# A fused attention and geglu kernel: three regroupings of maxima, copies and loads

## Chip, core and metric

The kernel runs on one core of a Trainium2 chip. The metric is the device time of one execution in microseconds, taken as the median of several runs; beside it stands one execution recorded by the hardware profiler, from which all rows come. In the rows PE is TensorE's matmuls and PEld its weight loads, DVE is VectorE, ACT ScalarE, POOL GpSimd and SP SyncE, which issues the DMAs.

## The reference

Sequence of 2048 tokens, width 576, 32 heads of 18, feed-forward width 4608, all in fp32.

```python
def _A_ref(x, wqkv, wo):                       # attention, H = 32, Dh = 18
    qkv = (x @ wqkv).reshape(B, S, 3, H, Dh).transpose(2, 0, 3, 1, 4)
    q, k, v = qkv[0], qkv[1], qkv[2]
    scores = jnp.einsum("bhqd,bhkd->bhqk", q, k) * (Dh ** -0.5)
    p = softmax(scores)
    o = jnp.einsum("bhqk,bhkd->bhqd", p, v)
    return o.transpose(0, 2, 1, 3).reshape(B, S, D) @ wo

def _B_ref(x, w_gate, w_up, w_down):           # geglu
    return (gelu(x @ w_gate) * (x @ w_up)) @ w_down

xn = layernorm(x)
out = x + _A_ref(xn, ...) * silu(_B_ref(xn, ...))
```

## The kernel before

**Values in two parts.** Each fp32 operand of the feed-forward and of the output projection is split into a high part that the matmul takes at full rate and a low part, the rest; a product is three matmuls (high by high, high by low, low by high). `split` and `cut` make these parts on the vector engines.

**Stages.** A prologue does the layer norm, q, k and v (to about 199 us). Then the feed-forward runs as 144 sections: four blocks of 512 tokens, in each 18 row groups r, in each two halves g. A section is 27 pairs of matmuls (`gate_up`, L423) into two PSUM banks, pg and pu, each pair with a gate row and an up row. Most sections share one pair of banks (tag "f"), so the next section's first matmul waits until `activate` has read them (L432, L433, L436, L437). After every second section, an even one, the products with w_down (`downs`, L534, in the first block also L521) are added into M on VectorE (L538, L523).

**Attention between the pairs.** Sections 0 to 10 are the lead: they carry the row maxima of the first unit of heads and queries and some of the second (`max_pair`: matmuls L767 into one of three ring buffers in PSUM, a reduce L768 on VectorE), four or five to a section from n=2 on. Sections 11 to 138 carry attention: eight score and eight maximum steps placed between the pairs by `spread`, then 32 value matmuls (L821), then the products of w_down where due. `spread` takes a number `tail`: so many of the specials are put behind the last pair instead of between pairs.

**Block changes.** Behind sections 35, 71 and 107 the next block's x is needed. It comes in three tiles `xd[k]`, each of a high and a low part, by DMA into partitions 0 to 63; `copy_xd` doubles them into partitions 64 to 127 (ScalarE the high part, GpSimd the low part). A slice (64x512) is a third of a tile. Pair 9k is the first that needs tile k, and hooks put work ahead of a pair by its number. `finish` ends a section: sums and cuts of the activations (L461, L451, L452) on GpSimd in the middle stretch. `sums_b` (L486 to L488) forms the sums of two row groups of w_down, and the pieces of these sums are stored; later blocks load them again (`t_piece`, L479).

**Epilogue.** Sections 139 to 143 carry no attention. The output projection runs between and behind them in 16 steps, one for each 128 tokens: `ready` splits the attention output (`split_o`) and computes the gate of the step after (`gate`: Tanh L944 on ScalarE, L945 on VectorE), `project_o` does the matmuls (L954), multiplies by the gate (L960) and adds x (L967); `load_xy` loads x and the feed-forward result yy of a later step. `load_wo` loads the output weights in five DMAs. `rec` is the reciprocal of the last unit's sums; its store (L848) is a task behind section 139.

**Order.** TensorE runs in program order, and so does SyncE from the attention on. The other engines are ordered by the planner of the framework, except that instructions marked `keep_in_program_order` keep theirs among themselves.

Of the kernel before, what the change touches and what calls it, by code (L numbers as in the profile page):

```python
# [10 lines left out]
AF = mybir.ActivationFunctionType  # L11
ALU = mybir.AluOpType
# [5 lines left out]
P = 128  # L18
# [5 lines left out]
HR = 64  # L24
NC = D // HR
XG = 3
NG = NC // XG
# [10 lines left out]
G = 2  # L38
# [24 lines left out]
def f(ap):  # L63
    return ap.bitcast(F32)
# [15 lines left out]
def kernel(ctx: ExitStack, tc: tile.TileContext, x, wqkv, wo, w_gate, w_up, w_down, out):  # L80
    nc = tc.nc
    x = x.rearrange("b s d -> (b s) d")
# [60 lines left out]
            out.append(t)  # L143
        return out

    def copy_xd(x, keep=lambda i: i, i=slice(None)):

        keep(nc.scalar.activation(x[0][HR:P, i], f(x[0])[0:HR, i], AF.Copy))
        keep(nc.gpsimd.tensor_copy(x[1][HR:P, i], x[1][0:HR, i]))  # L149


    def after(what, before, reason):
# [9 lines left out]
    with tc.tile_pool(name="pro", bufs=1) as pro, tc.tile_pool(name="pps", bufs=1, space=PSUM) as pps:  # L162
# [160 lines left out]
        t = ORDER[0]  # L323
# [29 lines left out]
        for b in range(NB):  # L353
# [43 lines left out]
    FF = {"w": ahead, "xd": XD, "down": [], "gates": [], "n": 0, "hooks": {}, "next": {}, "raw": {},  # L397
          "M": ffn.tile([P, 7, 2, DC], F32, name="M"),
          "A": [ffn.tile([P, 7, TH], F32R, name=m) for m in ("ah", "al")],
          "T": ffn.tile([P, 2, 7, DC], F32R, name="T")}  # L400
# [80 lines left out]
    def sums_b(raw):  # L481

        keep = tc.keep_in_program_order
        q = raw.rearrange("p g (c d) -> p (g c) d", c=2)
        t = ffn.tile([P, 5, DC], F32, name="tsum")
        keep(nc.gpsimd.tensor_tensor(t[:, 1:3], q[:, 0:4:2], q[:, 1:4:2], op=ALU.add))  # L486
        keep(nc.gpsimd.tensor_tensor(t[:, 3:5], q[:, 0:2], q[:, 2:4], op=ALU.subtract))
        keep(nc.gpsimd.tensor_tensor(t[:, 0], q[:, 0], q[:, 3], op=ALU.add))  # L488
        FF["b"] = q, t
# [79 lines left out]
    def section(specials=(), tag="f", slots=False, tail=0):  # L569

        n = FF["n"]
        FF["n"] += 1
        b, r = divmod(n // G, NR)
        g = n % G
        keep = tc.keep_in_program_order
        pairs, pg, pu = gate_up(tag)
        hooks, FF["hooks"], FF["next"] = FF["hooks"], FF["next"], {}

        def hook(i, what):
            hooks.setdefault(i, []).append(what)  # L580

        for i in range(n + 1, min(n + 3, NF)):
            if i not in FF["raw"]:
                FF["raw"][i] = load_gu(i % (NR * G))
        nxt = FF["raw"].pop(n + 1, None)
        one = split_ap if n + 1 < ATT.start else split
        if nxt:
            for k in range(NG - 1):
                split_gu(nxt, k, one)
        if n == 0:  # L590
            load_rawd(0)
        if g == 0 and (b, r) in FORMED:
            raw = FF["rawd"]
            hook(12, lambda: sums_b(raw))
        new = n + 1 < NF and (n + 1) % (NR * G) == 0
        xd = []
        if new:
            for k in range(NG - 1):
                hook(9 * k + 9, lambda k=k: xd.append(load_xd(b + 1, k)))
        for p in spread(pairs, specials, 1 if slots else None, hooks, tail):  # L600
            p()
        if nxt:
            split_gu(nxt, NG - 1, one)
        FF["w"] = nxt
        FF["act"] = activate(pg, pu, g, n < ATT.stop)
        if g > 0 or n not in ATT:
            FF.pop("last", lambda: None)()
        if new:
            xd.append(load_xd(b + 1, NG - 1))
            copy_xd(xd[0], keep)  # L610
            for k in range(1, NG):
                for i in range(XG):
                    FF["hooks"].setdefault(8 * k - 7 + 3 * i, []).append(lambda k=k, i=i: copy_xd(xd[k], keep, i))
            FF["xd"] = xd

    def downs(then={}):
# [93 lines left out]
    with tc.tile_pool(name="att", bufs=1, reuse_waits="tile") as att:  # L710
# [145 lines left out]
        for n, m in enumerate(FIRST):  # L856
            none = [lambda: None]
            lead = [lambda s=s: max_pair(*divmod(s, NS)) for s in range(slot, slot + m)]
            section((n == 2) * 5 * none + lead + (m > 0 and n != 2) * none, "ring" if n == 1 else "f",
                    tail=3 * (m > 0 and n % G == 0))  # L860
            if slot + m >= NS > slot:
                max_neg(0, tc.keep_in_program_order)
                max_store(0)
                FF["hooks"].setdefault(10, []).append(lambda: max_end(0))
            slot += m
            while n > 0 and chunk < KB and chunk * SLOTS <= slot + SLOTS:
                load_k(chunk)
                chunk += 1
            if n == 0:
                load_k(0)  # L870
                load_q(0)
            if n == 3:
                load_q(1)
            if n >= len(FIRST) - 2:
                load_v(n - len(FIRST) + 2)
            downs()
            finish()
        scaled = 0
        for n in range(NU * NA):
            u, i = divmod(n, NA)  # L880
# [31 lines left out]
    with tc.tile_pool(name="epi", bufs=1, reuse_waits="tile") as epi:  # L912
# [3 lines left out]
        def load_wo():  # L916
            keep = tc.keep_in_program_order
            nc.gpsimd.memset(f(OW[1])[HR:P, KT, :], 0.0)
            for i, w in enumerate(OW):
                keep(nc.sync.dma_start(f(w)[:, 0:KT, :], wos[i, 0:R0, :].rearrange("(k p) n -> p k n", p=P)))  # L920
                for a in range(2 - i):
                    keep(nc.sync.dma_start(f(w)[HR * a:HR * a + HR, KT, :], wos[i, R0:D, :]))
# [9 lines left out]
        def load_xy(b, j):  # L932

            rows = slice(b * TB + j * P, b * TB + (j + 1) * P)
            XY[b, j] = [epi.tile([P, D], F32, name=m, bufs=n) for m, n in (("xx", 4), ("yy", 3))[0:2 - (b == NB - 1)]]
            for t, a in zip(XY[b, j], (x, ys)):
                nc.sync.dma_start(t, a[rows, :])

        def gate(b, j):

            if b < NB - 1:
                yy = XY[b, j][1]
                th = epi.tile([P, D], F32, name="th")
                nc.scalar.activation(th, yy, AF.Tanh, scale=0.25)  # L944
                nc.vector.scalar_tensor_tensor(yy, th, 1.0, yy, op0=ALU.add, op1=ALU.mult)  # L945

        def project_o(b, j):

            po = ring("po")
            oh, ol = o = OP.pop((b, j))  # L950
            terms = [(k, x, w) for k in range(KT) for x, w in ((0, 0), (0, 1), (1, 0))] + [(KT, 0, 0), (KT, 0, 1)]
            for c in range(2):
                for m, (k, x, w) in enumerate(terms):
                    nc.tensor.matmul(po[:, c, 0:DC], o[x][:, k, :], OW[w][:, k, DC * c:DC * c + DC], start=(m == 0),  # L954
                                     stop=(m == len(terms) - 1))
            xx = XY[b, j][0]
            if b < NB - 1:
                t = XY[b, j][1]
                t2 = t.rearrange("p (c d) -> p c d", c=2)
                nc.vector.scalar_tensor_tensor(t2, t2, 0.25, po[:, :, 0:DC], op0=ALU.mult, op1=ALU.mult)  # L960
            else:
                t = epi.tile([P, D], F32, name="last", tag="yy", bufs=3)
                for c in range(2):
                    m = QUARTERS[2 * (j // 2) + c][2]
                    nc.vector.scalar_tensor_tensor(t[:, DC * c:DC * c + DC], FF["M"][:, m, j % 2], 0.25, po[:, c, 0:DC],
                                                   op0=ALU.mult, op1=ALU.mult)
            (nc.vector if (b, j) == groups[-1] else nc.gpsimd).tensor_tensor(xx, xx, t, op=ALU.add)  # L967
            outs.append((b * TB + j * P, xx))

        groups = [(b, j) for b in range(NB) for j in range(TB // P)]  # L970
        load_xy(*groups[0])
        load_wo()
        load_xy(*groups[1])
        n, outs = 0, []

        def ready():
            if n == len(groups):
                return
            b, j = groups[n]
            split_o(b, j)  # L980
            gate(b, j)
            if b < 2 and j == TB // P - 1:
                load_o(b + 2)

# [14 lines left out]
        for i in range(ENDS):  # L999
            section([], "ring" if i % 2 else "f")  # L1000
            if i == 1:
                ready()
            downs()
            finish()
            if i == 0:
                todo.pop("rec")[0]()
            if 0 < i <= NU - scaled:
                scale(scaled + i - 1)
                store_scale(scaled + i - 1)
            if i < NU - scaled:  # L1010
                load_scale(scaled + i)
            for k in range(GROUPS[i]):
                step()
# [4 lines left out]
        for i, c, m in QUARTERS:  # L1018
            t = ffn.tile([P, 2, DC], F32, name="tg", tag=("h0", "h1")[c], bufs=2 - c)
# [33 lines left out]
```

## Time and profile before

| | us |
|---|---|
| median of 3 runs | 2641.1 |
| lowest and highest | 2637.55 and 2644.84 |
| the profiled execution's own time | 2643.16 |
| its span | 2641.4 |
| its mean granted TensorE clock | 0.991 of full speed |

Busy shares of the span count time in which an instruction runs; matmuls are pipelined, and their ends are modelled. A row of a timeline gives start, duration, engine, line, operation, the tile written and the tiles read, a count where like instructions were joined, and in brackets the idle time of the engine before it and who ended that. The granted clock is the share of full speed that TensorE was allowed in a stretch of time.

### The profile page before, as it was taken

To read this page: it belongs to the slowest core of one execution; us is meant where nothing else is said; L and a number is where in the kernel's file an instruction comes from. 1 tells how busy PE (TensorE), PEld (TensorE's weight loads), DVE (VectorE), ACT (ScalarE), POOL (GpSimd) and SP (SyncE) were. 2 spreads that over 40 slices of the span, in tenths; PEclk is the share of its full clock that TensorE was granted. 3 is DMA by queue.
4 is the path that set the end of the run, shared out by engine and by line. 5 is a ranking of instruction groups with operands and counts; after the bars stand their busy time and mean duration, and the time that the engine had idled before them with its cause. 6 is when DMAs were issued, how large, how long until landed. Compare 5 with 4: busy or idle time off the path is not lost.

```text
span 2641.4 us, 52882 instructions
## 1 busy us (share of the span) xinstructions
PE 2572.5 (97%) x20548; PEld 1847.5 (70%) x20548; DVE 2164.7 (82%) x2459; ACT 1476.0 (56%) x1779; POOL 1580.3 (60%) x1603
## 2 busy tenths in 40 slices
PE   9999999999989999999999999999999999999988
PEld 8887766666656666666666666666666666667777
DVE  5325799999978988999988989888888988897467
ACT  3224366666667655555566655555566555555622
POOL 2115588888877855555566555555556555555642
PEclk9999999999999999999999999999999999999998
DMA  8875365555555566666675666555566655554683
GB/s 259 261 240 138 88 178 157 164 161 161 164 164 170 163 168 154 168 156 171 164 179 158 166 166 157 157 158 158 157 148 192 165 144 154 151 147 138 190 252 122
DMA packets 407881, 442.88 MB, mean 168 GB/s; under 512 B 106700, under 2 KB 286412, under 8 KB 407632
## 3 DMA queue, kind: packets, MB, share of 16 engines
q1 hardware_dynamic: 407632, 439.50, 60.3%
q8 instruction: 163, 2.67, 0.4%
q14 instruction: 86, 0.70, 0.1%
HBM read 344.12 MB, written 95.26 MB: 166 GB/s over the span
## 4 chain that ended last, share of the span: by engine, by line
PE 86%; DVE 7%; DMA 3%; ACT 1%; POOL 1%; issue 1%; SPq 1%; DVEq 0%; POOLq 0%; ACTq 0%
PE pg L423 20%; PE py L534 14%; PE acc L821 13%; PE pu L423 11%; PE pe L804 9%; PE pm L767 8%; PE po L183 7%; DVE mx L768 1%; DMA T<-ts 1%; PE po L954 1%; DVE m L777 1%; PE py L521 1%; DVE h L440 1%; DVE h L433 1%; DVE accs L827 1%
## 5 line engine op out<-in xcount | busy, mean ns | idle before, releaser
L805 ACT ACTIVATE pT<-pe 128x1024 f32<-128x1024 f32 x1024 | 1047.8, 1026 | 617.7 <-PE pe L804 583.6
L768 DVE TENSOR_REDUCE mx<-pm 128x2 f32<-128x1024 f32 x1024 | 1221.8, 1224 | 188.8 <-PE pm L767 170.3
L423 PE MATMUL pu<-xd,wh 64*128 64x512 f32 x2538 | 929.0, 397 | 6.8 <-POOL xd L149 5.2
L423 PE MATMUL pg<-xd,wh 64*128 64x512 f32 x2538 | 928.3, 397 | 4.7 <-ACT t L436 4.7
L423 PEld LDWEIGHTS pg<-xd,wh 64*128 64x128 f32 x2538 | 469.1, 185 | 120.5 <-issue 62.9
L423 PE MATMUL pg<-xd,wl 64*128 64x512 f32 x1269 | 497.3, 392 | 1.1 <-POOL wl L115 1.1
L423 PE MATMUL pu<-xd,wl 64*128 64x512 f32 x1269 | 497.0, 392 | 0.0
L423 PEld LDWEIGHTS pu<-xd,wh 64*128 64x128 f32 x2538 | 469.2, 185 | 35.1 <-POOL xd L149 6.8
L108 POOL TENSOR_SCALAR wh<-raw 128x384 fp32r<-128x384 f32 x402 | 214.5, 536 | 444.7 <-PE pu L423 313.4
L821 PE MATMUL acc<-pT,VS 128*32 128x512 f32 x4096 | 467.3, 597 | 0.0
L804 PE MATMUL pe<-QT,KA 64*128 64x512 f32 x2048 | 418.6, 398 | 21.1 <-DVE mx L768 8.6
L110 POOL TENSOR_TENSOR wl<-raw,wh 128x384 fp32r<-128x384 f32 x402 | 410.2, 1023 | 27.7
L767 PE MATMUL pm<-KA,QT 64*128 64x512 f32 x2048 | 416.1, 395 | 4.7 <-ACT pT L805 3.6
L534 PE MATMUL py<-T,ah 128*128 128x288 f32 x1876 | 385.5, 301 | 14.9 <-DMA T<-ts 9.3
L538 DVE TENSOR_TENSOR M<-py,M 128x576 f32<-128x576 f32 x448 | 339.0, 758 | 34.5 <-PE py L534 19.9
L534 PEld LDWEIGHTS py<-T,ah 128*128 128x128 f32 x1876 | 301.8, 190 | 70.1 <-issue 54.5
L452 POOL TENSOR_TENSOR al<-h,ah 128x512 fp32r<-128x512 f32 (+1 forms) x139 | 286.4, 2061 | 59.5 <-ACT ah L449 42.3
L821 PEld LDWEIGHTS acc<-pT,VS 128*32 128x32 f32 x4096 | 120.2, 110 | 277.9 <-issue 231.3
L804 PEld LDWEIGHTS pe<-QT,KA 64*128 64x128 f32 x2048 | 195.1, 184 | 144.8 <-DVE mx L768 32.9
L534 PE MATMUL py<-T,al 128*128 128x288 f32 x938 | 277.6, 296 | 0.0
L423 PEld LDWEIGHTS pg<-xd,wl 64*128 64x128 f32 x1269 | 235.2, 185 | 32.0 <-POOL wl L115 2.0
L423 PEld LDWEIGHTS pu<-xd,wl 64*128 64x128 f32 x1269 | 235.3, 185 | 14.4
(154 smaller groups left out, 2962.1 us busy)
## 6 DMA issues: line engine op xcount, KB each, us to landing
T<-ts SPq DMA_DIRECT2D x98, 576.0 KB
KA<-qk SPq DMA_DIRECT2D x768, 72.0 KB
T<-ts SPq DMA_DIRECT2D x98, 432.0 KB
raw<-in_B_w_gate_dram SPq DMA_DIRECT2D x144, 288.0 KB
raw<-in_B_w_up_dram SPq DMA_DIRECT2D x144, 288.0 KB
ts<-T SPq DMA_DIRECT2D x36, 576.0 KB
VS<-vs SPq DMA_DIRECT2D x128, 152.0 KB
qk<-t SPq DMA_DIRECT2D x72, 256.0 KB
```

The source lines that it names most:

```text
L108: first = nc.gpsimd.tensor_scalar(hi, raw, 1.0, 1.0, op0=ALU.mult, op1=ALU.mult)
L110: keep(nc.gpsimd.tensor_tensor(lo, raw, f(hi), op=ALU.subtract))
L183: nc.tensor.matmul(o, st, m, start=(i == 0), stop=(i == len(terms) - 1))
L423: nc.tensor.matmul(o, w[1 + wp][k][rr, c, :], xd[k][xp][rr, c, :], start=(i == 0), stop=(i == len(terms) - 1))
L452: keep(two.tensor_tensor(lo, raw, f(hi), op=ALU.subtract))
L534: nc.tensor.matmul(py[:, t, 0:DC], h[:, i, tt], T[:, w, k], start=n == 0, stop=n == 2)
L538: nc.vector.tensor_tensor(M[:, m], py[:, :, 0:DC], M[:, m], op=ALU.add)
L767: nc.tensor.matmul(pm[:, a], QS[u, r][rr, t * P:(t + 1) * P], KS[(u * NA + c) % KB][r][rr, :], start=True, stop=True)
L768: nc.vector.tensor_reduce(MX[u][:, 2 * r:2 * r + 2, t, c], pm, axis=AX.X, op=ALU.max)
L804: nc.tensor.matmul(pe[:, a], KS[(u * NA + c) % KB][r][rr, t * P:(t + 1) * P], QS[u, r][rr, :], start=True, stop=True)
L805: nc.scalar.activation(PT[u, kt][:, 2 * r:2 * r + 2, :], pe, AF.Exp, scale=SCALE)
L821: nc.tensor.matmul(ACC[u][32 * a:32 * a + 32, :], VS[(u * NA + c) % VB][:, v:v + 32], pt[:, a, :], start=first, stop=last, skip_group_chec ...
```

## The change

The diff regroups work in three stages.

In the lead, the last three specials of a section (two maxima and an empty one) are placed behind the pairs in sections with odd n instead of even n.

At a block change, `copy_xd` gets an argument for the part. Before, tile 0 was copied whole at the end of the old block's last section, tile 1 in slices ahead of pairs 1, 4 and 7, and tile 2 in slices ahead of pairs 9, 12 and 15, on both engines. After, ScalarE copies tiles 0 and 1 whole at the section's end, and tile 2 in slices ahead of pairs 4, 8 and 12; GpSimd copies all nine slices at the section's end, ahead of the sums of `finish`. The hook of `sums_b` goes from 12 to 22 in a block's first section that has one (r == 0).

In the epilogue, the loads of the output weights and of the first two steps' x and yy are given out behind section 139, after its `finish` and before the store of rec, instead of ahead of section 139. `gate` moves from `ready` into `project_o`, one step later. The adds of L967 run on VectorE in all steps; before, GpSimd did them in all but the last.

```diff
-    def copy_xd(x, keep=lambda i: i, i=slice(None)):
+    def copy_xd(x, part, keep=lambda i: i, i=slice(None)):
 
-        keep(nc.scalar.activation(x[0][HR:P, i], f(x[0])[0:HR, i], AF.Copy))
-        keep(nc.gpsimd.tensor_copy(x[1][HR:P, i], x[1][0:HR, i]))
+        if part == 0:
+            keep(nc.scalar.activation(x[0][HR:P, i], f(x[0])[0:HR, i], AF.Copy))
+        else:
+            keep(nc.gpsimd.tensor_copy(x[1][HR:P, i], x[1][0:HR, i]))
...
             raw = FF["rawd"]
-            hook(12, lambda: sums_b(raw))
+            hook(22 if r == 0 else 12, lambda: sums_b(raw))
...
         if new:
             xd.append(load_xd(b + 1, NG - 1))
-            copy_xd(xd[0], keep)
-            for k in range(1, NG):
+            for k in range(2):
+                copy_xd(xd[k], 0, keep)
+            for i in range(XG):
+                FF["hooks"].setdefault(4 + 4 * i, []).append(lambda i=i: copy_xd(xd[NG - 1], 0, keep, i))
+            for k in range(NG):
                 for i in range(XG):
-                    FF["hooks"].setdefault(8 * k - 7 + 3 * i, []).append(lambda k=k, i=i: copy_xd(xd[k], keep, i))
+                    copy_xd(xd[k], 1, keep, i)
             FF["xd"] = xd
...
             section((n == 2) * 5 * none + lead + (m > 0 and n != 2) * none, "ring" if n == 1 else "f",
-                    tail=3 * (m > 0 and n % G == 0))
+                    tail=3 * (m > 0 and n % G == 1))
...
             xx = XY[b, j][0]
+            gate(b, j)
             if b < NB - 1:
...
-            (nc.vector if (b, j) == groups[-1] else nc.gpsimd).tensor_tensor(xx, xx, t, op=ALU.add)
+            nc.vector.tensor_tensor(xx, xx, t, op=ALU.add)
             outs.append((b * TB + j * P, xx))
 
         groups = [(b, j) for b in range(NB) for j in range(TB // P)]
-        load_xy(*groups[0])
-        load_wo()
-        load_xy(*groups[1])
         n, outs = 0, []
...
             b, j = groups[n]
             split_o(b, j)
-            gate(b, j)
             if b < 2 and j == TB // P - 1:
...
             finish()
             if i == 0:
+                load_wo()
+                load_xy(*groups[0])
+                load_xy(*groups[1])
                 todo.pop("rec")[0]()
```

## The prediction

> **What bounds the kernel now.** I read the page first, then windows by stage, then what the matmuls waited for, then timelines around the places that the diff touches. The page's first row, and the chain that ended last by engine:
>
> ```profile
> PE 2572.5 (97%) x20548; PEld 1847.5 (70%) x20548; DVE 2164.7 (82%) x2459; ACT 1476.0 (56%) x1779; POOL 1580.3 (60%) x1603
> PE 86%; DVE 7%; DMA 3%; ACT 1%; POOL 1%; issue 1%; SPq 1%; DVEq 0%; POOLq 0%; ACTq 0%
> ```
>
> TensorE is busy for 97% of the span. The diff leaves its matmuls as they are, so it can move the 3% of idle time and the time lost to a lower granted clock, and nothing else. Where these lie shows in windows of the lead, of the sections of attention up to the first block change, of two block changes and of the epilogue (start:end, length, then busy time of PE, PEld, DVE, ACT and POOL with instructions, granted clock, DMA share, GB/s):
>
> ```profile
> 212.00:333.00 121.00, 109.21 (x854) 90.71 (x856) 92.81 (x109) 43.75 (x76) 64.61 (x56) 1.00 0.43 111
> 333.00:742.00 409.00, 408.24 (x3408) 279.84 (x3404) 372.09 (x403) 271.97 (x314) 336.77 (x323) 1.00 0.57 163
> 742.00:786.00 44.00, 34.96 (x244) 23.39 (x236) 31.48 (x31) 23.73 (x29) 36.09 (x34) 0.92 0.55 153
> 1361.00:1400.00 39.00, 33.86 (x242) 23.77 (x236) 30.01 (x30) 21.50 (x25) 26.50 (x27) 0.91 0.71 197
> 2501.00:2641.40 140.40, 116.88 (x848) 108.12 (x846) 102.19 (x132) 31.82 (x45) 46.48 (x38) 0.91 0.63 196
> ```
>
> In the sections between block changes nothing is left to win (0.8 us idle in 409). The lead idles 11.8 us, the two block changes 9.0 and 5.1 us, the epilogue 23.5 us, and in the last three the clock sags too. Those are the three places of the diff. The waits of TensorE (what waited, who released it: total us, times, the longest):
>
> ```profile
> PE py L534 <- DMA T<-ts: 9.3, 1, 9.3
> PE pu L423 <- POOL xd L149: 5.2, 3, 3.7
> PE py L534 <- DVE M L538: 4.7, 1, 4.7
> PE py L521 <- DVE mx L768: 3.1, 5, 0.6
> ```
>
> One wait for a piece of w_down's sums (T), three for GpSimd's copies of x, 3.7 the longest, one for a VectorE add in the epilogue, and five short ones in the lead.
>
> **Part 1, the lead: +8 us.** Four reduces follow in each section of four maxima; with the tail, three of them stand on VectorE in front of L433 and L437, which read the section's two PSUM banks. An even section (n=4) ends so, then the end of an odd one (n=5):
>
> ```profile
> 244.32 0.39 PE L423 MATMUL pu<-xd,wh 64*128 64x512 f32 x1
> 244.56 0.63 PE L767 MATMUL pm<-KA,QT 64*128 64x512 f32 x3
> 244.52 3.49 DVE L768 TENSOR_REDUCE mx<-pm 128x2 f32<-128x1024 f32 x3 [1.96 <-PE pm L767]
> 248.52 0.68 DVE L437 TENSOR_TENSOR t<-t,pg 128x512 f32<-128x512 f32 x1
> 245.80 0.53 PE L521 MATMUL py<-T,ah 128*128 128x288 f32 x2 [0.62 <-DVE mx L768]
> ...
> 259.44 0.39 PE L423 MATMUL pu<-xd,wh 64*128 64x512 f32 x1
> 261.90 0.49 PE L423 MATMUL pu<-xd,wh 64*128 64x512 f32 x1 [0.40 <-DVE t L437]
> ```
>
> In n=4 the pairs end at 244.71 (244.32 + 0.39), and L437 gives the banks back at 249.20 (248.52 + 0.68): 4.49 us later. It costs nothing, since w_down's matmuls (L521) run meanwhile; they wait only 0.62 for a ring buffer. In n=5, without a tail, the next section goes on at 261.90, 2.07 us behind the end of its pairs at 259.83. Nothing but the next section follows an odd one, and that needs the two banks. So with the tail there, TensorE resumes 4.49 instead of 2.07 behind the pairs, +2.4. Two maxima, four matmuls in some 0.5 us (by x3 in 0.63), leave the pairs and run inside the gap: +2.0 net. Odd sections with maxima are n=3, 5, 7, 9: **+8.0**. Gone are the five waits of L521, **-3.1**. What is late next is the odd section's Tanh and sums; their products are read only behind the following even section, some 10 us on, and cost nothing.
>
> The gap may also cost clock. Of its 4.0 us behind the tail's maxima one matmul fills 0.5. What such gaps did in two other places (windows of about one step of the clock, as above):
>
> ```profile
> 776.70:780.10 3.40, 1.26 (x12) 0.74 (x10) 3.40 (x3) 0.76 (x1) 3.40 (x3) 1.00 0.02 5
> 780.10:783.50 3.40, 3.40 (x20) 2.67 (x18) 1.86 (x3) 2.05 (x2) 3.40 (x4) 0.51 0.00 0
> ...
> 281.80:285.20 3.40, 2.32 (x22) 1.57 (x18) 2.66 (x3) 1.05 (x2) 1.83 (x2) 1.00 0.35 104
> ```
>
> After 1.26 busy of 3.40 the next 3.40 run at 0.51, which loses 3.40 x 0.49 = 1.7 us. At 2.32 busy of 3.40, in the lead, the windows beside it keep 1.00. A gap of 4.0 with 0.5 busy lies nearer the first, but part of it can fall into two such windows and part of a slow stretch may run beside another wait; between 0 and 1.7 I take half, 0.85 x 4 = **+3.4**. The lead: 8.0 - 3.1 + 3.4 = **+8** (bounds +5 and +12).
>
> The Trainium skill ("TensorE: Matmul & The Clock Gate", its part on the clock gate) lets the clock fall only after a whole idle window of about 3.4 us; by that the lead would come to +5, since the matmul in the gap breaks it. The rows above differ from it: 1.26 us of work stood in the window ahead of the slow one.
>
> **Part 2, block changes: -10 us.** At the first (n=36 begins near 742), GpSimd, ScalarE and TensorE, then TensorE at the second, and the window behind each of the two waits:
>
> ```profile
> 743.68 1.73 POOL L149 CAST xd<-xd 64x512 fp32r<-64x512 f32 x3 [0.47 <-DMA xd<-xhs]
> 749.59 2.94 POOL L452 TENSOR_TENSOR al<-h,ah 128x1280 fp32r<-128x1280 f32 x1
> 758.12 0.79 POOL L488 TENSOR_TENSOR tsum<-rawd 128x288 f32<-128x288 f32 x1
> 758.97 0.60 POOL L149 CAST xd<-xd 64x512 fp32r<-64x512 f32 x1
> 742.82 0.60 ACT L825 ACTIVATE accs<-acc 128x512 f32<-128x512 f32 x1
> 744.73 0.63 ACT L148 ACTIVATE xd<-xd 64x512 fp32r<-64x512 f32 x1
> 759.63 0.79 PE L423 MATMUL pu<-xd,wh 64*128 64x512 f32 x1 [3.73 <-POOL xd L149]
> ...
> 1370.33 0.55 PE L423 MATMUL pu<-xd,wh 64*128 64x512 f32 x1 [1.28 <-POOL xd L149]
> ```
> ```profile
> 759.65:763.10 3.45, 3.45 (x17) 1.05 (x21) 1.91 (x2) 1.11 (x2) 2.98 (x4) 0.51 0.55 174
> 1370.70:1374.10 3.40, 3.40 (x20) 2.65 (x18) 1.42 (x2) 2.47 (x3) 3.23 (x6) 0.51 1.05 320
> ```
>
> The last slice copy (758.97) stands on GpSimd behind the unit's sums (L452 ends at 752.5) and the sums of the next rows of w_down (L488 ends at 758.9). The last pair waits 3.73 for it, and the stretch after it runs at 0.51: 3.45 x 0.49 = 1.7. Both go once the nine slices stand ahead of all that: -5.4. At the second change the wait is 1.28 and a slow stretch follows: -3.0. The third has neither. ScalarE copies one slice in 0.63 between its Exps, six in that section; now three, and one whole tile at the section's end, by the slice's price at most 1.9: 3 x 0.63 less against 1.9 more, no more than an Exp's worth of pace: -0.5 each, -1.6. Sum **-10**.
>
> Bounds. The whole copy of xd[1] now lies ahead of L825 and the first Exp: up to 1.5 late at each change, -10 + 4.5 = -5.5. All nine copies on GpSimd before the sums: six of 0.6 move in front, 3.5 us, so that L452 ends near 756; the products that read it stand behind the last pair (755.7, without the stall) and 32 value matmuls, near 759. That covers it, by about 3 us, and sums_b behind pair 22 lies behind L452 and has no reader before them. The copies also stand at their landings: the second tile's was 743.68, the third's no row shows, and it lies between there and 758.97.
>
> **Part 3, the epilogue: -9 us.** SyncE's queue, TensorE, ScalarE and VectorE in order of time, a window, and the group of GpSimd's adds:
>
> ```profile
> 2499.53 0.37 SPq L937 DMA_DIRECT2D xx<-in_A_x_dram  x1
> 2503.95 0.54 SPq L937 DMA_DIRECT2D yy<-ys  x1
> 2509.62 3.94 SPq L479 DMA_DIRECT2D T<-ts  x3
> 2523.62 0.61 PE L534 MATMUL py<-T,ah 128*128 128x288 f32 x1 [9.35 <-DMA T<-ts]
> 2574.78 0.68 ACT L944 ACTIVATE th<-yy 128x576 f32<-128x576 f32 x1 [5.73 <-DMA yy<-ys]
> 2577.72 0.82 PE L534 MATMUL py<-T,ah 128*128 128x288 f32 x2 [4.67 <-DVE M L538]
> 2637.71 0.76 DVE L967 TENSOR_TENSOR xx<-xx,last 128x576 f32<-128x576 f32 x1
> ```
> ```profile
> 2523.60:2531.20 7.60, 7.58 (x43) 7.58 (x44) 5.14 (x7) 0.00 (x0) 4.55 (x7) 0.73 0.62 107
> ```
> ```profile
> L967 POOL TENSOR_TENSOR xx<-xx,yy 128x576 f32<-128x576 f32 x12 | 21.5, 1795 | 41.9 <-DVE yy L960 41.9
> ```
>
> Three T pieces are issued at 2509.62, behind nine DMAs issued from 2499.53 to 2504.5 and behind the next weights, and the second product waits until 2523.62. Moved ahead of these nine, T is asked for about 5 us (the nine issues) earlier and has the transfers to itself; it comes before the 2514.3 at which it is needed (2523.62 - 9.35). Then the 9.35 go and the 0.73 clock behind it, 7.58 x 0.27 = 2.0: -11.4 at best. What is late next is wo, which the first projection reads right behind those matmuls, 7.58 x 0.73 = 5.5 us on, near 2520. The bytes are the same and begin at the same time, so that all of them are there by 2523.6 at the worst, where the projection now starts at 2531.2: -7.6 at least. I take **-9**. The rec store stays behind the same DMAs.
>
> The gates: each Tanh L944 waits for its yy and stands in ScalarE's queue ahead of work for the products. In project_o it is given out a section or a step later; but ScalarE's order is the planner's, which can put it ahead of the section's Square all the same. For the first gate I count that as a rival; the 4.67 at 2577.72 behind the Tanh that waited 5.73 I leave standing (0, bound -6.7: 4.67 and the 2.0 of clock as above).
>
> The adds: 12 of 1.8 us leave GpSimd, 12 of 0.76 go to VectorE, 9.1 us in the epilogue's window where it has 38 idle. That slack hides them; uncovered, at most 9.1 on the chain. I take 0.
>
> **Sum:** 8 - 10 - 9 = -11 against the profiled execution's 2643.2 (span 2641.4 and 1.8 around it), 2632. That execution lies 2.1 above the runs' median of 2641.1, so 2630 as a median.
>
> **Rivals.** (B) The first gate's Tanh keeps its place ahead of section 140's Square and waits for yy, which is now the last but one to land, by about 2521 to 2523.6. The products then stand by their adds on VectorE as at 2577.72; of the epilogue about -3.5 is left (9.35 + 2.0 less a wait like the 5.73 and its clock): 2643.2 + 8 - 10 - 3.5 - 2.1 = 2636. For it: the trace has two such Tanh waits ahead of other work; against: it is emitted behind that Square now. 0.18.
>
> (C) The gates move for good, and the 4.67 with its slow clock goes too: 2630 - 6.7 = 2623. For it: that Tanh was emitted ahead of the section that it holds up, and now is behind it. Against: the planner's freedom. 0.20.
>
> (D) Slower. GpSimd, at each block change, stands at the landing of the third tile, with the unit's sums behind it. Place: the products after section 36, 72 and 108, which read L452. If that tile lands as late as the last copy ran (758.97 + 0.6), L452 comes 5.5 us on (three sums of 1.3, 1.3 and 2.9), at 765, some 6 behind the products' 759, and 1.7 of clock on top: 3 x 7.7 = +23 in place of nothing, less 8.4 for the stalls gone: +15. 2643.2 + 15 + 8 - 9 - 2.1 = 2655. It decides from a landing at about 753 on. For it: the DMA share is 0.55 to 1.05 in these windows. Against: the second tile was there at 743.68, and the third is asked for no later than 9 pairs after it. 0.14.
>
> (E) The planner leaves the copies where they were, behind the sums, so that the change doesn't do what it says there; the move of sums_b alone then gives about 3: 2643.2 + 8 - 3 - 9 - 2.1 = 2637. For it: copies wait for a landing and the sums don't. Against: the diff keeps both in program order. 0.08.
>
> **How the numbers follow.** Forecast 0.40, 2630, with a range of its own of 2624 to 2636 from the bounds of its terms. A measurement of this kernel tells 0.3%, 7.9 us, from no change: faster is below 2633.2, slower above 2649.0. Faster: 0.30 of the forecast, all of C, 0.02 of B: 0.52. The same: 0.10 of the forecast, 0.16 of B, 0.07 of E: 0.33. Slower: D and 0.01 of E: 0.15. The range from 2615 (C with the lead's lower bound and the epilogue's full 11.4) to 2647 (the lead at +12 with B and blocks at -5.5) leaves out most of D and little else.
>
> **What would show it.** Lead: in sections 3, 5, 7, 9 pu at L423 waits for L437 about 2.4 us longer than 0.40, the five waits of L521 for the reduces are gone, and the lead's window is some 5 to 12 us longer. Blocks: no wait for POOL xd L149 and clock 1.00 in the stretch after; D would show as py L534 waiting for al at L452. Epilogue: no py wait for T, wo's or yy's wait below 2 us. The prediction is wrong if the lead's window isn't longer, or if the epilogue's products still wait over 5 us.

## The result: slower by 0.22%, with the profile after

| | before | after |
|---|---|---|
| median of 20 runs each, us | 2638.55 | 2644.61 |
| lowest and highest, us | 2632.43 to 2644.84 | 2641.56 to 2648.05 |
| ratio to before, 95% interval | | 1.0022 (1.0015 to 1.0029) |
| span of the profiled execution, us | 2641.4 | 2643.9 |
| its mean granted clock | 0.991 | 0.990 |

The forecast was 11 us down; it went 6 us up. The two profiled executions differ by only 2.5 us, since the one of before lies 4.6 above its median of 20 and the one of after 1.4 above its own.

Lines move by two to six in the changed kernel: L432, L437, L538, L768, L929, L944 and L945 of before are L434, L439, L540, L773, L934, L949 and L950; in the experiments' kernels they move a little further.

The page's first row after the change:

```profile
PE 2576.6 (97%) x20548; PEld 1853.5 (70%) x20548; DVE 2161.6 (82%) x2474; ACT 1473.7 (56%) x1773; POOL 1554.9 (59%) x1594
```

To see where the time went, both traces are cut at the same events: the Square (L432, after the change L434) of sections 1 and 12, 35 and 39, 71 and 75, 107 and 111, then 139 and the end. Columns are start:end, length, then busy time (instructions) of PE, PEld, DVE, ACT and POOL, granted clock, DMA share, GB/s. Before:

```profile
211.91:351.29 139.38, 127.50 (x1012) 102.62 (x1016) 108.55 (x124) 58.20 (x92) 82.40 (x73) 1.00 0.45 118
739.03:822.71 83.68, 73.82 (x560) 48.14 (x563) 61.73 (x64) 53.39 (x67) 67.10 (x65) 0.96 0.59 167
1358.57:1435.95 77.38, 72.11 (x560) 48.82 (x556) 60.29 (x64) 49.65 (x61) 49.89 (x52) 0.96 0.71 190
1974.15:2050.14 75.99, 71.08 (x560) 47.82 (x556) 60.57 (x64) 49.67 (x60) 49.76 (x52) 0.98 0.69 193
2507.92:2641.40 133.48, 109.96 (x790) 102.51 (x786) 95.34 (x126) 31.13 (x44) 44.38 (x35) 0.91 0.61 187
```

After:

```profile
210.55:360.24 149.69, 133.89 (x1012) 107.85 (x1016) 110.50 (x124) 58.17 (x91) 82.34 (x73) 0.93 0.41 110
748.29:829.26 80.97, 73.48 (x560) 48.18 (x563) 60.80 (x64) 52.71 (x65) 67.22 (x66) 0.96 0.60 173
1365.65:1439.28 73.63, 69.31 (x560) 45.87 (x556) 60.60 (x64) 48.94 (x59) 50.18 (x54) 1.00 0.74 199
1978.26:2053.92 75.66, 71.27 (x560) 47.40 (x556) 60.46 (x64) 48.92 (x58) 49.65 (x53) 0.98 0.70 193
2510.65:2643.90 133.25, 110.72 (x790) 102.55 (x786) 91.01 (x142) 31.45 (x45) 16.67 (x19) 0.91 0.60 189
```

In this pair of profiles the lead is 10.3 us longer, the three block changes differ by -2.7, -3.8 and -0.3, the epilogue by -0.2. The lead's clock fell from 1.00 to 0.93; the epilogue got nothing. The profiles of the experiments below, cut at the same events, show how far one pair can be trusted. The lead is 139.4 to 141.3 us long with the old tail and 148.5 to 150.3 with the new one (six profiles each), +9 on the mean. The block changes differ by -3.9, -1.6 and -0.5 on the mean (three profiles with the old copies, six with the new), so the -3.8 at the second is mostly chance. The epilogue is 131.9 to 135.1 without its edits (three profiles) and 131.5 to 133.6 with them (four).

TensorE's waits in the changed kernel (what waited, who released it: total us, times, longest):

```profile
PE pu L425 <- DVE t L439: 11.5, 4, 2.9
PE py L536 <- DVE M L540: 10.1, 3, 9.1
...
PE po L959 <- DVE ol L934: 5.6, 2, 4.6
PE pg L425 <- ACT t L438: 2.8, 4, 0.7
...
PE pu L425 <- POOL xd L151: 2.0, 1, 2.0
PE po L959 <- DVE oh L935: 1.9, 1, 1.9
```

The wait for T is gone, and so are the five of the lead's products. In their place stand 11.5 us for L439 in the lead and 10.1 for the adds into M; 2.0 of the wait for the copy of x remains.

**The lead.** The end of section 3 in the changed kernel, in order of time (start, duration, engine, line):

```profile
231.81 3.49 DVE L773 TENSOR_REDUCE mx<-pm 128x2 f32<-128x1024 f32 x3 [1.96 <-PE pm L772]
233.18 0.49 PE L425 MATMUL pg<-xd,wh 64*128 64x512 f32 x1 [0.70 <-ACT t L438]
235.81 0.68 DVE L439 TENSOR_TENSOR t<-t,pg 128x512 f32<-128x512 f32 x1
236.55 0.79 PE L425 MATMUL pu<-xd,wh 64*128 64x512 f32 x1 [2.88 <-DVE t L439]
```

Three reduces hold VectorE until 235.3, L439 ends at 236.49, and only then does the second matmul of the next section run. Three windows there, of one step of the clock each:

```profile
231.36:234.77 3.41, 1.61 (x11) 0.75 (x7) 2.96 (x3) 1.09 (x2) 0.84 (x1) 1.00 0.61 201
234.77:238.19 3.42, 1.64 (x8) 1.36 (x10) 2.42 (x4) 1.50 (x3) 0.16 (x1) 0.50 0.68 149
238.19:241.60 3.41, 3.41 (x20) 2.67 (x18) 1.23 (x1) 0.91 (x3) 3.05 (x3) 0.50 0.00 0
```

The gap straddles two windows, each with 1.6 us of work, and each is followed by one at half clock (0.50 in the second and third rows). Behind section 7 it is the same, with 1.83 and 1.41 us of work. Behind sections 5 and 9 only the second window (1.26 and 0.67) is followed by half clock; the first (1.99 and 2.55) is not. The four gaps thus bring six slow windows.

**The block changes.** GpSimd and TensorE at the first, then GpSimd at the second:

```profile
753.01 1.72 POOL L151 CAST xd<-xd 64x512 fp32r<-64x512 f32 x3 [2.23 <-DMA xd<-xhs]
...
760.50 2.90 POOL L454 TENSOR_TENSOR al<-h,ah 128x1280 fp32r<-128x1280 f32 x1
763.46 1.72 POOL L151 CAST xd<-xd 64x512 fp32r<-64x512 f32 x3
764.12 0.79 PE L425 MATMUL pu<-xd,wh 64*128 64x512 f32 x1 [2.01 <-POOL xd L151]
...
1373.33 1.72 POOL L151 CAST xd<-xd 64x512 fp32r<-64x512 f32 x3
1375.14 2.95 POOL L454 TENSOR_TENSOR al<-h,ah 128x1280 fp32r<-128x1280 f32 x1
1378.15 1.72 POOL L151 CAST xd<-xd 64x512 fp32r<-64x512 f32 x3
```

At the first change the third tile's slices still run behind the unit's sums (L454 ends at 763.4), though the program hands them out first. At the second they do so too; there only the second tile's slices (1373.33) have come ahead of the last of the sums, and no pair waits. At the third change the third tile's slices run behind the sums both before and after, and nothing waits for them.

**The epilogue.** SyncE, ScalarE, VectorE and TensorE around the products of section 140, then a row of SyncE's own waits:

```profile
2511.74 0.34 SPq L942 DMA_DIRECT2D yy<-ys  x1
2516.81 0.32 SPq L942 DMA_DIRECT2D yy<-ys  x1
2523.09 0.68 ACT L949 ACTIVATE th<-yy 128x576 f32<-128x576 f32 x1 [5.80 <-DMA rT<-rec]
2523.81 0.76 DVE L950 SCALAR_TENSOR_TENSOR yy<-th,yy 128x576 f32<-128x576 f32 x1 [4.99 <-ACT th L949]
2525.22 0.58 ACT L434 ACTIVATE h<-pgu 128x512 f32<-128x512 f32 x1
2526.62 0.75 DVE L540 TENSOR_TENSOR M<-py,M 128x576 f32<-128x576 f32 x1
2527.52 0.82 PE L536 MATMUL py<-T,ah 128*128 128x288 f32 x2 [9.07 <-DVE M L540]
```

```profile
SPq L942 <- DMA woh<-wos: 3.7, 1, 3.7
```

Both gates' Tanhs stand on ScalarE ahead of the section's Square (L434), and their VectorE halves ahead of the first add into M (L540). The first Tanh starts only at 2523.09: its yy was issued at 2511.74, behind the output weights. (The row names another DMA that landed about then; in the pinned kernel below the same Tanh is released by yy.) The products stop for 9.07 us, where T had stopped them for 9.35.

**The end.** VectorE and TensorE in the last projections:

```profile
2623.26 2.09 DVE L1026 SCALAR_TENSOR_TENSOR M<-tg,M 128x576 f32<-128x576 f32 x3
2625.26 0.69 DVE L934 TENSOR_TENSOR ol<-KA,oh 128x512 fp32r<-128x512 f32 x1
...
2626.00 0.61 PE L959 MATMUL po<-woh,ol 128*128 128x288 f32 x1 [4.62 <-DVE ol L934]
```

The split for the 14th step now comes wholly behind three gates of M, and the wait of 2.94 at this place became 4.62.

### The profile page after: what moved, and what is told of

Same layout as the page of the kernel before. It is cut to its first block, busy times and chain, and to the rows that moved or that the text cites. A ratio compares the mean times of both kernels' runs of the same rounds, so it can differ in the third digit from the quotient of the medians.

```text
span 2643.9 us, 52874 instructions
## 1 busy us (share of the span) xinstructions
PE 2576.6 (97%) x20548; PEld 1853.5 (70%) x20548; DVE 2161.6 (82%) x2474; ACT 1473.7 (56%) x1773; POOL 1554.9 (59%) x1594
## 4 chain that ended last, share of the span: by engine, by line
PE 86%; DVE 7%; DMA 3%; ACT 2%; POOL 1%; issue 1%; SPq 0%; POOLq 0%; ACTq 0%; DVEq 0%
PE pg L425 19%; PE py L536 14%; PE acc L826 13%; PE pu L425 12%; PE pe L809 9%; PE pm L772 8%; PE po L185 7%; DVE mx L773 2%; PE po L959 2%; PE py L523 1%; DVE m L782 1%; DMA KA<-qk 1%; DVE h L435 1%; DVE accs L832 1%; DVE h L442 1%
## 5 line engine op out<-in xcount | busy, mean ns | idle before, releaser
L773 DVE TENSOR_REDUCE mx<-pm 128x2 f32<-128x1024 f32 x1024 | 1222.2, 1224 | 195.2 <-PE pm L772 181.0
L425 PE MATMUL pu<-xd,wh 64*128 64x512 f32 x2538 | 932.6, 399 | 13.6 <-DVE t L439 11.5
L536 PE MATMUL py<-T,ah 128*128 128x288 f32 x1876 | 383.8, 300 | 10.5 <-DVE M L540 10.1
L540 DVE TENSOR_TENSOR M<-py,M 128x576 f32<-128x576 f32 x448 | 338.9, 757 | 29.9 <-PE py L536 15.3
L454 POOL TENSOR_TENSOR al<-h,ah 128x512 fp32r<-128x512 f32 (+1 forms) x139 | 286.3, 2060 | 67.9 <-ACT ah L451 58.1
```

What stands on the lines that cost most here:

```text
L425: nc.tensor.matmul(o, w[1 + wp][k][rr, c, :], xd[k][xp][rr, c, :], start=(i == 0), stop=(i == len(terms) - 1))
L454: keep(two.tensor_tensor(lo, raw, f(hi), op=ALU.subtract))
L536: nc.tensor.matmul(py[:, t, 0:DC], h[:, i, tt], T[:, w, k], start=n == 0, stop=n == 2)
L540: nc.vector.tensor_tensor(M[:, m], py[:, :, 0:DC], M[:, m], op=ALU.add)
L773: nc.vector.tensor_reduce(MX[u][:, 2 * r:2 * r + 2, t, c], pm, axis=AX.X, op=ALU.max)
```

## The experiments

Ratios are to the kernel before, run beside each on the same chip; microseconds are worked out from them. "Lead", "blocks" and "epilogue" mean the three parts of the diff.

### The lead alone, on the kernel before

```diff
-                    tail=3 * (m > 0 and n % G == 0))
+                    tail=3 * (m > 0 and n % G == 1))
```

> The kernel before with the lead's edit alone (the tail in odd sections). Theory: the lead's edit alone costs about +10 us: four odd sections resume about 2.0 us later net, less 3.1 for the waits gone, and two to six windows of half clock add some 6; so a ratio near 1.004, and pu waits four times about 2.9 us for L437. Rival: the lead's edit costs only the +5 of the waits (1.002) and the rest of the lead's 10 us in the changed kernel comes from elsewhere. Second rival: no cost (1.000), the profile's lead was disturbed.

Measured: 1.0042 (1.0029 to 1.0056), +11 us; median 2652.88 against 2639.78. Of its waits:

```profile
PE pu L423 <- DVE t L437: 11.5, 4, 2.9
```

The same 11.5 us in four waits as in the changed kernel: the cost is this edit's and needs no other part.

### The changed kernel without the lead's edit

```diff
-                    tail=3 * (m > 0 and n % G == 1))
+                    tail=3 * (m > 0 and n % G == 0))
```

> The changed kernel with the lead's tail put back into even sections. Theory: the lead is the whole loss, and blocks and epilogue together give a gain: about -10 us against the changed kernel, -4 against the kernel before (ratio near 0.9985). Rival: lead and the other two are not additive because the clock's windows shift, and it stays within 2 us of the changed kernel.

Measured: 0.9979 (0.9970 to 0.9988), -5.5 us against before and some 11 below the changed kernel's 1.0022. The lead is more than the whole loss, and it adds to the rest.

### The blocks alone, on the kernel before

The lead, the loads, the gates and the adds as before; the copies and the hook of `sums_b` as in the diff.

```diff
-            copy_xd(xd[0], keep)
-            for k in range(1, NG):
+            for k in range(2):
+                copy_xd(xd[k], 0, keep)
+            for i in range(XG):
+                FF["hooks"].setdefault(4 + 4 * i, []).append(lambda i=i: copy_xd(xd[NG - 1], 0, keep, i))
+            for k in range(NG):
                 for i in range(XG):
-                    FF["hooks"].setdefault(8 * k - 7 + 3 * i, []).append(lambda k=k, i=i: copy_xd(xd[k], keep, i))
+                    copy_xd(xd[k], 1, keep, i)
```

> The kernel before with the block changes' edits alone (copies and the hook of sums_b). Theory: they give the 6 to 7 us that the section times show at the three block changes, so -6 against the kernel before (ratio 0.9977). Rival: part of what the section times show there is the clock's windows falling otherwise, which changes from run to run, and it is -3 (0.9989).

Measured: 0.9973 (0.9963 to 0.9983), -7 us. The stage lengths above add up to -6.8 in the pair of profiles and to -6.0 on the mean; the rival's -3 lies outside the interval.

### The epilogue alone, on the kernel before

```diff
             xx = XY[b, j][0]
+            gate(b, j)
...
-            (nc.vector if (b, j) == groups[-1] else nc.gpsimd).tensor_tensor(xx, xx, t, op=ALU.add)
+            nc.vector.tensor_tensor(xx, xx, t, op=ALU.add)
...
-        load_xy(*groups[0])
-        load_wo()
-        load_xy(*groups[1])
...
-            gate(b, j)
...
             if i == 0:
+                load_wo()
+                load_xy(*groups[0])
+                load_xy(*groups[1])
```

> The kernel before with the epilogue's edits alone (loads behind section 139, gates in project_o, adds on VectorE). Theory: the wait for T goes and the wait for the adds behind the gate takes its place: within 2 us of the kernel before (ratio 0.9993 to 1.0007). Rival: the epilogue's edits give the 3 to 5 us that I allowed for that case (0.9985).

Measured: 1.0000 (0.9991 to 1.0009). Of its waits:

```profile
PE py L534 <- DVE M L538: 9.9, 3, 8.3
```

No wait for T, and one of 8.3 for the adds: taken and given back. The rival's 0.9985 lies outside the interval. The product of the three parts' ratios, 1.0042 x 0.9973 x 1.0000, is 1.0015, on the edge of the changed kernel's interval; no interaction is needed to explain it.

### The changed kernel with the loads back in their old place

```diff
         groups = [(b, j) for b in range(NB) for j in range(TB // P)]
+        load_xy(*groups[0])
+        load_wo()
+        load_xy(*groups[1])
...
             if i == 0:
-                load_wo()
-                load_xy(*groups[0])
-                load_xy(*groups[1])
```

> The changed kernel with the output weights' and the first two steps' loads back ahead of section 139, gates and adds as changed. Theory: the move of the loads did take the 9.3 us wait for T away, and the gate's place took it back: here the wait for T of about 9 us returns, the wait for the adds falls below 3 us, and the time stays within 3 us of the changed kernel (ratio to the kernel before about 1.002). Rival: the loads' move is harmful by itself, since yy comes later by it, and this kernel is 5 us or more faster than the changed one.

Measured: 1.0011 (1.0002 to 1.0020), some 3 us below the changed kernel's ratio, intervals overlapping. Of its waits:

```profile
PE py L536 <- DMA T<-ts: 7.4, 2, 6.9
...
PE py L536 <- DVE M L540: 4.1, 1, 4.1
```

T is late again, by 6.9, and the long wait for the adds is gone; the 4.1 is that of the second such stop, later in the epilogue. The move of the loads exchanges one wait for another.

### The gates pinned behind the section's work

`behind(a, b)` only keeps `a` after `b` in their engine's order.

```diff
-                nc.scalar.activation(th, yy, AF.Tanh, scale=0.25)
-                nc.vector.scalar_tensor_tensor(yy, th, 1.0, yy, op0=ALU.add, op1=ALU.mult)
+                behind(nc.scalar.activation(th, yy, AF.Tanh, scale=0.25), FF["tanh"])
+                behind(nc.vector.scalar_tensor_tensor(yy, th, 1.0, yy, op0=ALU.add, op1=ALU.mult), FF["add"])
```

Here `FF["tanh"]` is L438's instruction of the last section and `FF["add"]` the last add into M, both as the program has handed them out.

> The changed kernel with each gate's Tanh ordered behind the Tanh of the section before it in the program, and the gate's VectorE instruction behind the last add into M. Theory: the 9.1 us in which the products wait for their adds behind L950 in the epilogue come from the gate's place, not from the transfers: the wait falls below 2 us, and with the slow clock behind it the kernel gains 9 to 11 us against the changed kernel (ratio to the kernel before near 0.998). Rival: the output weights are not there before about 2523, so that the first projection waits instead and only 3 to 5 us are gained.

Measured: 0.9993 (0.9984 to 1.0002), -7.7 us against the changed kernel's 1.0022, short of the 9 to 11 expected. ScalarE and VectorE at the products of section 140, and two of TensorE's waits:

```profile
2517.55 0.58 ACT L438 ACTIVATE h<-pgu 128x512 f32<-128x512 f32 x1
2519.69 0.75 DVE L544 TENSOR_TENSOR M<-py,M 128x576 f32<-128x576 f32 x1
2523.13 0.68 ACT L953 ACTIVATE th<-yy 128x576 f32<-128x576 f32 x1 [2.70 <-DMA yy<-ys]
```

```profile
PE po L963 <- DVE ol L938: 6.2, 3, 4.8
PE py L540 <- DVE M L544: 4.3, 4, 2.1
```

The first Tanh runs at 2523.13, no sooner than in the changed kernel (2523.09), so its transfer is as late as it was. But the Square and the adds no longer stand behind it, and the products wait 2.1 instead of 9.07. The output weights were in time: the first projection runs at 2526.16, and no wait of po is for them. So it was the order on two engines that made a late transfer hold the products. Whether loading the first yy ahead of the output weights would have done as well was not run.

### The large sum kept behind the nine copies

```diff
-            eng.tensor_tensor(h[:, 4:6], h0[:, 0:2], h[:, 0:2], op=ALU.add)
+            first = eng.tensor_tensor(h[:, 4:6], h0[:, 0:2], h[:, 0:2], op=ALU.add)
+            if FF["n"] % (NR * G) == 0 and FF["n"] < NF:
+                tc.keep_in_program_order(first)
```

> The changed kernel with the first large sum of a new block's last unit kept behind GpSimd's nine copies, so that the third tile's copies run before it. Theory: the 2.0 us wait for GpSimd's copy at the first block change and the slow clock behind it go, -3 to -4 us there; the second and third block changes stay as they are. Rival: the third tile lands late, GpSimd stands at its landing with the sums behind it, and the products of section 36 wait for L454, 0 to +5 us.

Measured: 1.0023 (1.0014 to 1.0033), no difference from the changed kernel that this can tell. GpSimd at the first block change, and that stage's window:

```profile
758.32 1.72 POOL L151 CAST xd<-xd 64x512 fp32r<-64x512 f32 x3 [0.17 <-DMA xd<-xhs]
760.12 1.29 POOL L463 TENSOR_TENSOR h<-h,h 128x512 f32<-128x512 f32 x1
```

```profile
748.67:827.54 78.87, 71.94 (x560) 46.83 (x563) 62.59 (x64) 52.67 (x65) 67.31 (x66) 0.96 0.62 177
```

The copies now run ahead of the sum, and the wait of 2.01 is gone. The stage is 78.87 instead of 80.97 long; the medians don't confirm these 2 us, and the five other profiles with these copies not pinned have 79.7 to 80.0 there, so that the pin is worth nearer 1 us than 2. The third tile had landed when its copies came up, but for 0.17, and nothing waited for the later sums: the rival of a late tile is out.

### The adds back on GpSimd

```diff
-            nc.vector.tensor_tensor(xx, xx, t, op=ALU.add)
+            (nc.vector if (b, j) == groups[-1] else nc.gpsimd).tensor_tensor(xx, xx, t, op=ALU.add)
```

> The changed kernel with the adds of the epilogue back on GpSimd (but for the last). Theory: the adds' engine is no part of the loss: within 2 us of the changed kernel. Rival: the adds on VectorE are what puts the split of the next group behind the gates of M at the end, where the last projections now wait 4.6 instead of 2.9; with the adds on GpSimd that wait is 2.9 again and the kernel is 2 to 4 us faster.

Measured: 1.0013 (1.0004 to 1.0022), within 2.4 us of the changed kernel and with an overlapping interval. Of its waits:

```profile
PE py L536 <- DVE M L540: 14.2, 2, 9.0
...
PE po L959 <- DVE oh L935: 2.9, 1, 2.9
```

The last projections wait 2.9 again, as the rival has it, but a second stop of 5.2 behind a gate (14.2 less 9.0) is back, which the changed kernel did not have. The 1.91 for a split has gone as well. The adds' engine shifts the planner's order in several places with about the same price in sum; the time alone does not tell the theory (within 2) from the rival (2 to 4).

### What the experiments point to

The lead as before, the gates pinned, the copies ahead of the large sum; loads and adds as in the diff.

> The lead's tail as before, the gates behind the Tanh and the adds of the section before, and the block changes' copies ahead of the unit's large sum; the loads and adds as in the changed kernel. Theory: the parts add up: -10 (lead), -8 (gates) and 0 to -2 (copies) against the changed kernel, about 2626, ratio to the kernel before 0.995. Rival: the transfers and the clock's windows shift and half of the gates' gain is lost: 0.997 to 0.998.

Measured: 0.9936 (0.9923 to 0.9948), median 2625.74 against 2641.43, -17 us. The expectation's parts, -10 and -8 from +6, make -12. By the measured ratios (0.9979 without the lead's edit, 0.0029 less by the pinned gates) it would be 0.9950, -13, just outside the interval; where the other 4 come from was not taken apart.

Then the split for the 14th step ahead of the gates of M:

```diff
         M = FF["M"]
+        split_o(*groups[n + 1])
         for i, c, m in QUARTERS:
```

> The joined kernel with the split of the 14th group ahead of the gates of M at the end. Theory: the wait of 4.7 us of the last projections for that split goes, with up to 3.4 us of slow clock behind it: -4 to -7 us against the joined kernel (ratio to before about 0.993). Rival: the last projections need M's gates one step later anyway, through the three ring buffers, and only 1 to 2 us go.

Measured: 0.9918 (0.9904 to 0.9931), median 2620.96, another 4.8 us. VectorE and TensorE at that place, then the epilogue's window, from section 139's Square to the end:

```profile
2600.11 0.68 DVE L940 TENSOR_TENSOR ol<-KA,oh 128x512 fp32r<-128x512 f32 x1
2600.85 0.40 PE L965 MATMUL po<-woh,ol 128*128 128x288 f32 x1 [2.77 <-DVE ol L940]
2601.14 2.09 DVE L1034 SCALAR_TENSOR_TENSOR M<-tg,M 128x576 f32<-128x576 f32 x3
```

```profile
2498.26:2617.30 119.04, 104.75 (x790) 96.24 (x786) 91.36 (x142) 31.07 (x45) 17.66 (x19) 1.00 0.66 212
```

The split now precedes the gates, and the wait is 2.77 instead of 4.8 in the joined kernel; it has not gone, as the expectation had it. The epilogue takes 119.0 us where the joined kernel's profile has 127.4 and before and after have 133, at a clock of 1.00 where these have 0.95 and 0.91. This kernel beats both by about 0.8% and 1.0%.

## Why the prediction was wrong, step by step

**The lead (+8): the mechanism right, one term too small.** The reduces hold L437 as worked out: the second matmul came 0.70 + 0.49 + 2.88 us behind the tail, 4.1, where the prediction had 4.0. The waits came out as summed too: 11.5 + 2.8 at the starts of sections against 4.7 + 1.6 + 3.1 before is +4.9, the prediction's 8.0 less 3.1; smaller waits lost 1, so that TensorE idled 3.9 longer. The stage grew by 10.3 in the pair of profiles and by 9 on the mean, and the edit alone cost +11. The rest is the clock, for which 3.4 stood in the sum: TensorE's busy time for the same 1012 matmuls rose by 6.4 in the pair (127.50 to 133.89) and by 5.3 on the mean. I took half of one slow window for each gap; there were six for four gaps. By the rule of the Trainium skill that the prediction cites ("TensorE: Matmul & The Clock Gate", its part on the clock gate: a whole idle window) the lead would have been +5. The trace disagrees: the windows with 1.6 us of work above were not idle, and 0.50 followed.

**The blocks (-10): -7, the step "both go once the nine slices stand ahead of all that".** The nine slices did not stand ahead at any of the three changes: the third tile's ran behind L454 each time. At the first, 2.0 of the wait of 3.73 stayed so, with a slow window behind it (0.54 from 763.60 to 767.00): -2.7 in this profile, -3.9 on the mean, where -5.9 stood. At the second the wait of 1.28 did go, since the second tile's slices moved ahead of L454 and nothing waited for the third's; the -3.8 of this profile next to the -3.5 of the sum is luck, as the mean is -1.6. Rival E named the cause ("the planner leaves the copies where they were") and was set aside with "the diff keeps both in program order". Marked instructions do not all keep their order among themselves, as the account of the kernel has it: the mark only puts an instruction behind the one handed out just before it. The sums' large add has no mark, so it and what hangs on it could pass the copies; the pinned kernel shows it by taking the wait away.

**The epilogue (-9): 0. This is the step that turned the sign.** What the prediction said of T came true: no wait for it is left. "For the first gate I count that as a rival" is where it failed: rival B was the case, and its condition was in the rows of before, where a Tanh that waited 5.73 stood ahead of a Square. B's price was wrong too, 3.5 left of the gain against none. I let the products stop for a wait like the 5.73; two gates stood in front, not one, the first yy, issued at 2511.74 behind the output weights, was there only at 2523.09, and SyncE had stood 3.7 for one of these weights ahead of the second yy (2516.81). The wait of 9.07 is also one of the two signs that the prediction named for being wrong. The argument "all of them are there by 2523.6 at the worst", so at least 7.6, counted the transfers alone and said nothing of the adds in the queue. Of the transfers the pinned kernel bears it out as far as it reaches: the first yy was there at 2523.13, and the output weights for the first projection at 2526.16.

**The second stop in the epilogue (0).** The 4.67 behind a Tanh did go, but not as in rival C. That Tanh still stands ahead of the Square (2578.17 and 2578.76) and waits 5.27 for its yy; the products came up only at 2578.46, where before they did at 2571.21, and so missed most of it. With the adds back on GpSimd the stop is there again with 5.2, with the loads back with 4.1. Besides, 1.91 came for another split, and 2.94 became 4.62 at the end. **The adds (0)** hold: no difference in the medians that can be told, waits exchanged.

**The sum.** With the measured terms, +11 for the lead, -7 for the blocks and 0 for the epilogue, it is +4, and the medians show +5.8 by the ratio. The median it was set on, 2641.1 of three runs, was 2.5 above that of 20; it changes the level, not the sign. The measured 2644.6 lies within the range, since its upper end is nearly the case that came, the lead and the blocks near their bad bounds together with B. With the prediction's own terms that end is 2643.2 + 12 - 5.5 - 3.5 - 2.1 = 2644, not 2647, and the lower end is 2618, not 2615. The forecast itself stood on an epilogue's gain that did not come.

## What to carry to other kernels

When a transfer is taken off the critical path, look at what stands in the in-order queues behind the next transfer to be late: a gate that waits for its data ahead of a Square can cost as much as the stall that went. Program order that is promised for single instructions is no chain; where one link is free, the planner moves it, so pin the work that must not pass. A tail of reduces is free only behind a section that is followed by other work for the matmuls; here each gap of about 4 us brought one or two windows of half clock besides. And one pair of profiles is a thin base for a stage of 75 us: the -3.8 above was -1.6 over several.

## What the runs showed of the chip

A window of 3.41 us with 1.61 busy, in which no idle stretch was as long as the window, was followed by half clock (0.50). In the changed kernel's lead all windows with 1.83 us of work or less were followed by half clock, those with 1.99 or more by full speed. TensorE's busy time there rose by 5 to 6 us for the same matmuls, beside 4 us more of idle time. In the last kernel the epilogue ran at 1.00 instead of 0.91 and was 14 us shorter, and its same 790 matmuls kept TensorE busy for 104.75 us instead of 110.72: some 6 of the 14 came from the clock, not from the stops themselves.
